# Moving one unit's loads forward in a fused RWKV-6 and feed-forward kernel, and reordering a few steps around it

## The chip, the cores and the metric

The kernel runs on one core of one Trainium2 chip. The metric is the device time of one execution in microseconds, as a median of several runs. The profile shows one execution; its span (675.3 us here) is a little shorter than the time of a run (677.92 us), because the run counts start and end as well.

## What is computed

Two blocks follow each other. The first is a linear attention with a state of 48 x 48 per head, 4 batches, 8 heads, 768 tokens:

```python
for t in range(S):
    cur = einsum('bhd,bhe->bhde', u * k[t], v[t])
    y[t] = einsum('bhd,bhde->bhe', r[t], state + cur)
    state = w[t][..., None] * state + einsum('bhd,bhe->bhde', k[t], v[t])
```

The second takes these outputs as x, 3072 tokens of 384 channels, through a feed-forward layer with weights of 384 x 2048 and 2048 x 384:

```python
h = x @ w_in
g = h * (1.0 / (1.0 + exp(-h)))
out = g @ w_out
```

All is in float32.

## The kernel before

The work is cut into 12 **units**, each of 128 tokens of two batches. In a unit the decays are multiplied up in seven levels, so that the recurrence becomes matrix products: at each level l the queries `tr` and keys `tk` are scaled by products `tw` of decays (VectorE and GpSimd), TensorE makes scores, and VectorE keeps the masked part of them. Then follow the outputs `yt`, the state's update, and the copies that bring `yt` into the layout of x (`xt`). The feed-forward layer of a unit runs on TensorE while the next unit's attention steps run on the other engines. While the first units run, the weights are rounded in 16 pieces ("piece": two steps on ScalarE, called head and tail, one join on VectorE, one add on GpSimd).

The loads of a unit from the third on come in blocks of 32 tokens. One call of `load_blocks` makes four transfers, and a unit needs twelve calls, so 48 transfers, all issued on the sync engine's queue:

```python
def load_blocks(i, name, g):
    n, b0 = units[i]
    src, t0 = {"w": w, "r": r, "k": k}[name], n * L + g * 32
    room = raw[:, i % NSLOT, WRK[name]]...          # two slots: units share one by parity
    for e in range(2):
        for a in range(2):
            nc.sync.dma_start(out=room[...], in_=src[...])

def block_loads(i):
    return [(load_blocks, i, name, g) for name in "wkr" for g in range(4)]
```

The same queue carries the weights, the outputs, the values, the tokens for the bonus term, its diagonal and the copies of x:

```python
def load_weight(i): ...; nc.sync.dma_start(out=dst, in_=src)         # L178
def load_rk(i): ...                                                  # L90, tokens for the bonus term
def bonus_sum(i, x): ...                                             # own_sums on VectorE, then at x == 1:
    for b in range(NB):
        for s in range(2):
            nc.sync.dma_start(out=diag[i][b][s::2], in_=own_sums[...])   # L423

def move_x(i):                                                       # ten transfers, L711
    xt[i] = pt.tile([128, KC, TU], F32, name="xt")
    for h in range(H):
        ...
        nc.sync.dma_start(out=xt[i][...], in_=yt[i][...])

def down(i, b, part, parts=4):                                       # unit 0's second product, in parts
    ...
    if part == parts - 1:
        nc.vector.tensor_copy(out=ob_b, in_=po[i, b])
        nc.sync.dma_start(out=out[row0:row0 + L, :], in_=ob_b)       # L777
```

Steps that the reading of the profile comes back to:

```python
def scores(i, l, *between):                 # products on TensorE (L525), then keep (L535) on VectorE
    ...
    if i < NTOK and grow: grow_queries(i, l)            # L471, VectorE
    do(*between)
    for e in range(2): keep(e)
def bonus_spread(i): ... ScalarE copies diag to both_b (L439, L441); VectorE shuffles it (L442)
def bonus_write(i):  ... copy_predicated into score (L448)
def turn(i, b, name): nc.vector.transpose(...)          # L336, raw -> tw, tk, tr
def turn_k(i, b):  transposes on TensorE; nc.scalar.copy(out=kq[i, b], in_=p_tr)     # L636
def y_state(i, b): p_yt = ps.tile(..., name="p_m", bufs=2); matmuls with state       # L648
def up(i, m):      12 matmuls xt, w_in -> p_h (L752); Silu on ScalarE (L758)
def sums(i, m), weight_sums(which): VectorE adds that prepare the second product     # L797, L789
def quarter(i, which): one of seven products of the second layer -> p_o, two buffers
                                                        # L815, evicted on VectorE, L824
```

From unit 3 on the order is regular: `mix(i)` gives thirteen groups of attention steps, and between them stand seven `quarter` steps of unit i - 2 and eight `up` steps of unit i - 1. The first three units are ordered by hand. The part that the change touches most, before:

```python
for m in range(6):
    do((piece, 10 + m), *others[m])          # unit 2's start; others[5] begins with (clear, 1)
...
others = {2: [(level, 2, 2), (prepare, 2, 3), (weight_sums, 1), (sums, 1, 0), (down, 0, 0, 3), (down, 0, 1, 0), (bonus, 2, 0),
              (bonus_sum, 2, 0)],
          3: [(burst, 2, 3), (keep_level, 2, 3), (keep_level, 2, 4), (go_on, 2, 4), (prepare, 2, 5), (down, 0, 1, 1),
              (bonus, 2, 1), (bonus, 2, 2), (load_rk, 3), (sums, 1, 1), (down, 0, 1, 2), (bonus_sum, 2, 1)],
          4: [(down, 0, 1, 3)],
          5: [(burst, 2, 5), ..., (bonus_spread, 2), (bonus_write, 2), (load_values, 3), (weight_sums, 2)],
          6: [(up, 1, 7), (sums, 1, 2)]}
loads = block_loads(3) + block_loads(4)
for l in range(2, NL):
    do(*others[l], *loads[(l - 2) * len(loads) // 5:(l - 1) * len(loads) // 5])
do(*both(turn_k, 2), (sums, 1, 3), *both(y_state, 2), *both(y, 2), (weight_sums, 3), *both(update, 2), (move_x, 2))
```

`clear(1)` sets the unused columns of the slot that units 1 and 3 share to zero; it has to come before unit 3's loads.

Of the kernel before, what the change touches and what calls it, by code (L numbers as in the profile page):

```python
# [38 lines left out]
def kernel(  # L39
# [11 lines left out]
    nc = tc.nc  # L51
# [4 lines left out]
    NL = 7  # L56
# [11 lines left out]
    NTOK = 2  # L68
# [387 lines left out]
    def odd_keys(i, l):  # L456

        c, blocks = 1 << l, NP * (L >> (l + 2))
        nc.scalar.copy(out=keys(i, X[(l + 1) % 2] * L + c, [4 * c, blocks], [c, 2], [1, c]),  # L459
                       in_=keys(i, NP * L + c, [4 * c, blocks], [NP * L + c, 2], [1, c]))  # L460
# [7 lines left out]
    def grow_queries(i, l):  # L468
        c = 1 << l
        odd = tr[i].rearrange("p q (i s c) -> p q i s c", s=2, c=c)[:, :, :, 1, :]  # L470
        nc.vector.tensor_tensor(out=odd, in0=odd, in1=tw[i][l][:, :, 0::2][:, :, :, None].to_broadcast([128, Q, L >> (l + 1), c]),  # L471
                                op=ALU.mult)
# [44 lines left out]
    def score_products(i, l, queries, sc):  # L517
        c, ni = 1 << l, L >> (l + 1)

        for p in range(NP):  # L520
            for e in range(2):
                rows = slice(PD * e, PD * e + D)

                apart, r_p, s_p = 2 * (NP - p) - 1, queries[rows, p, :], sc[e][:, p, :]
                nc.tensor.matmul(bass.AP(tensor=s_p.tensor, offset=s_p.offset,  # L525
                                         ap=[s_p.ap[0], [apart * L // 2, 2], [1, L // 2]]),
                                 lhsT=tk[i][rows, X[l % 2] + p, :],
                                 rhs=bass.AP(tensor=r_p.tensor, offset=r_p.offset + c,
                                             ap=[r_p.ap[0], [apart * L, 2], [2 * c, ni], [1, c]]),
                                 start=True, stop=True)  # L530

    def keep_masked(i, l, e, sc):
        c, ni = 1 << l, L >> (l + 1)
        dst = score[:, i % NSC, e].rearrange("p (b q) (i s c) -> p b q i s c", b=NB, s=2, c=c)[:, :, :, :, 1, :]
        nc.vector.copy_predicated(out=dst, mask=masks[l][:, :, None].to_broadcast([128, NB, NP, ni, c]),  # L535
                                  data=sc[e].rearrange("p (b q) (i c) -> p b q i c", b=NB, c=c))

    def scores(i, l, *between):
        c, ni = 1 << l, L >> (l + 1)

        name = "p_h" if i == 0 and l % 2 == 1 else "p_sc"
        sc = [ps.tile([128, Q, L // 2], F32, name=name, bufs=2) for e in range(2)]
        score_products(i, l, tr[i], sc)
        if i < NTOK and l + 2 < NL:
            odd_keys(i, l + 1)

        def keep(e):
            if (i, l, e) in COPIED:

                for b in range(NB):  # L550
                    for x in range(ni):
                        first = 2 * x * c if b == 0 else L - (2 * x + 1) * c
                        rows, columns = slice(first, first + c), slice((2 * x + 1) * c, (2 * x + 2) * c)
                        nc.scalar.copy(out=score[rows, i % NSC, e, b * NP:(b + 1) * NP, columns],
                                       in_=sc[e][rows, b * NP:(b + 1) * NP, x * c:(x + 1) * c])
                return
            keep_masked(i, l, e, sc)


        grow = l + 1 < NL or units[i][0] > 0  # L560
        if i < NTOK and grow:
            grow_queries(i, l)
        do(*between)
        for e in range(2):
            keep(e)
        if i >= NTOK and grow:
            grow_queries(i, l)

    def level(i, l):
        if l + 1 < NL:  # L570
            odd_keys(i, l)
        scores(i, l)
        grow_keys(i, l)
        add_weight()
# [140 lines left out]
    def both(fn, i, *args):  # L715
        return [(fn, i, b, *args) for b in range(NB)]

    def block_loads(i):
        return [(load_blocks, i, name, g) for name in "wkr" for g in range(4)]
# [122 lines left out]
    def do(*steps):  # L842
        for fn, *args in steps:
            fn(*args)
# [7 lines left out]
    def back(fn, i, *args):  # L852
# [8 lines left out]
    blocks = block_loads(2)  # L861
    others = {1: [(clear, 0), (beat, 6)], 2: [(turn, 1, 0, "r"), (head_weight, 0), (beat, 2)],
              3: [(turn, 1, 1, "r"), (head_weight, 1), (beat, 2)], 4: [(turn, 1, 1, "w"), (reverse_v, 0)],
              5: [(bonus_spread, 0), (bonus_write, 0), (turn, 1, 0, "w")], 6: [*both(turn_in, 1, "k"), *blocks[0:4], (tail_weight, 0)]}
    between = {4: [(bonus_sum, 0, 1)]}
    for l in range(1, NL):
        do((scores, 0, l, *between.get(l, ())), *[(grow_keys, 0, l + 1)] * (l + 1 < NL), *others[l])
# [2 lines left out]
       *blocks[4:8], (product, 1, 0), (tail_weight, 1), (turn_k, 0, 0), (join_weight, 1), (dense_x, 0, 0), (turn_k, 0, 1),  # L870
       *both(turn, 1, "k"), (dense_x, 0, 1), (grow_queries, 1, 0), (odd_ones, 1), (tail_weight, 2), (head_weight, 2),
       *blocks[8:12], (start_keys, 1, nc.gpsimd, True), (add_weight,), (up, 0, 0), (join_weight, 2),
       (start_keys, 1, nc.gpsimd, False), (add_weight,), (tail_weight, 3), (head_weight, 3), (odd_keys, 1, 1), (grow_keys, 1, 1),
       (scores, 1, 1, (join_weight, 3)), (add_weight,), (up, 0, 1), (tail_weight, 4), (grow_keys, 1, 2), (head_weight, 4),
       (up, 0, 2))


    others = {1: [], 2: [(bonus_sum, 1, 0), (bonus_sum, 1, 1), (load_rk, 2), *both(update, 0)],
              3: [(bonus_spread, 1), (reverse_v, 1), (load_values, 2)], 4: [(bonus_write, 1)], 5: []}

    def piece(i):

        do(*[(head_weight, i + 1)] * (i + 1 < 2 * NW), (join_weight, i), (add_weight,), *[(tail_weight, i + 1)] * (i + 1 < 2 * NW))

    for m in range(1, 5):
        do((piece, m + 3), (scores, 1, m + 1), *[(grow_keys, 1, m + 2)] * (m + 2 < NL), (up, 0, m + 2), *others[m])

    do((scores, 1, NL - 1), (head_weight, 9), (join_weight, 8), (add_weight,), (up, 0, 7), *both(y, 1), (turn_apart, 1),
       (tail_weight, 9), *both(turn_k, 1), *both(dense_x, 1), (piece, 9), *both(update, 1), (up, 1, 0), *both(turn, 2, "w"))

    others = {0: [(up, 1, 1), (down, 0, 0, 0), *both(turn, 2, "k"), (product, 2, 0), (product, 2, 1)],
              1: [(up, 1, 2), *both(turn, 2, "r"), *[(product, 2, l) for l in range(2, NL)]],
              2: [(down, 0, 0, 1), (odd_ones, 2), (start_keys, 2, nc.gpsimd, True), (grow_queries, 2, 0)],
              3: [(up, 1, 3), (start_keys, 2, nc.gpsimd, False), (reverse_v, 2)], 4: [(level, 2, 1), (up, 1, 4)],
              5: [(clear, 1), (down, 0, 0, 2), (up, 1, 5), (weight_sums, 0)]}
    for m in range(6):
        do((piece, 10 + m), *others[m])
    rounding.close()
    second.append(ctx.enter_context(tc.tile_pool(name="po", bufs=1, space=bass.MemoryType.PSUM)))

    others = {2: [(level, 2, 2), (prepare, 2, 3), (weight_sums, 1), (sums, 1, 0), (down, 0, 0, 3), (down, 0, 1, 0), (bonus, 2, 0),
                  (bonus_sum, 2, 0)],
              3: [(burst, 2, 3), (keep_level, 2, 3), (keep_level, 2, 4), (go_on, 2, 4), (prepare, 2, 5), (down, 0, 1, 1),
                  (bonus, 2, 1), (bonus, 2, 2), (load_rk, 3), (sums, 1, 1), (down, 0, 1, 2), (bonus_sum, 2, 1)],
              4: [(down, 0, 1, 3)],
              5: [(burst, 2, 5), (keep_level, 2, 5), (keep_level, 2, 6), (go_on, 2, 6), (up, 1, 6), (bonus_spread, 2),
                  (bonus_write, 2), (load_values, 3), (weight_sums, 2)],
              6: [(up, 1, 7), (sums, 1, 2)]}
    loads = block_loads(3) + block_loads(4)
    for l in range(2, NL):  # L910
        do(*others[l], *loads[(l - 2) * len(loads) // 5:(l - 1) * len(loads) // 5])
    do(*both(turn_k, 2), (sums, 1, 3), *both(y_state, 2), *both(y, 2), (weight_sums, 3), *both(update, 2), (move_x, 2))

    ROOM = 1, 1, 2, 1, 1, 1, 1, 1, 2, 1, 2, 1, 0
    for i in range(3, len(units)):
# [39 lines left out]
```

## Time and profile before

| | |
|---|---|
| time, median of 3 runs | 677.92 us (677.67 to 677.95) |
| span of the profiled execution | 675.3 us |
| TensorE (PE) busy | 648.6 us, 96% |
| VectorE (DVE) busy | 435.7 us, 65% |
| GpSimd (POOL) busy | 280.4 us, 42% |
| ScalarE (ACT) busy | 202.8 us, 30% |
| granted TensorE clock, mean | 0.982 |
| DMA | 49.21 MB, mean 73 GB/s |

A profile line of a timeline gives the start, the duration, the engine, the line of the kernel, the operation with out<-in, and how often it follows itself; in square brackets stands how long the engine was idle before it, and who released it. "SPq" is the sync engine's DMA queue: its durations are the time that the issuing takes, not the transfer. A line of windows gives the busy time of every engine in one stretch, and the granted clock of TensorE, where 1.00 is full speed. Busy time of TensorE counts slow matmuls as busy too, so a stretch at half clock looks busy and does half the work.

### The profile page before, as it was taken

Reading aid. Unit: us, or ns where it says so; the run is one execution under the profiler, and the core shown is the slowest. Engines: PE = TensorE matmul, PEld = TensorE weight load, DVE = VectorE, ACT = ScalarE, POOL = GpSimd, SP = SyncE. Lnnn points to the kernel's source line nnn. Section 1 sums busy time; section 2 is a strip of 40 time slices with the busy share of each in tenths; the row PEclk is TensorE's granted clock in tenths of the full one; section 3 lists DMA queues with packets and bytes.
Section 4 is the critical chain, followed back from the end, with each engine's and each line's share of the span. In section 5 each row is a group of like instructions: output and inputs, shape, how many; then the busy total and the mean of one; then the engine's idle time right before and its main releaser. Section 6 shows DMA issues by size and latency. Waiting matters only on the chain.

```text
span 675.3 us, 12894 instructions
## 1 busy us (share of the span) xinstructions
PE 648.6 (96%) x4878; PEld 585.1 (87%) x4878; DVE 435.7 (65%) x737; ACT 202.8 (30%) x408; POOL 280.4 (42%) x356
## 2 busy tenths in 40 slices
PE   8989999877599999999999999999999999999998
PEld 7877875777389989989989989989989989989997
DVE  6889779766147757757757757658658656653131
ACT  6787871210032132132132132123123133122110
POOL 6887489243205425425425425434434434330000
PEclk9999999889599999999999999999999999999999
DMA  9857911443353441441351451451451121100000
GB/s 235 252 92 225 239 50 26 81 74 48 64 106 52 70 86 33 68 90 33 62 96 31 64 98 28 64 96 29 65 96 32 33 49 26 47 2 24 23 1 24
DMA packets 201134, 49.21 MB, mean 73 GB/s; under 512 B 188912, under 2 KB 195952, under 8 KB 201072
## 3 DMA queue, kind: packets, MB, share of 16 engines
q1 hardware_dynamic: 199488, 47.79, 34.9%
q10 hardware_dynamic: 1584, 0.59, 0.4%
q8 instruction: 39, 0.64, 0.4%
q14 instruction: 23, 0.19, 0.1%
HBM read 39.52 MB, written 4.72 MB: 66 GB/s over the span
## 4 chain that ended last, share of the span: by engine, by line
PE 81%; DVE 7%; SPq 6%; issue 2%; ACT 2%; POOL 2%; DMA 1%; DVEq 0%; POOLq 0%; ACTq 0%
PE p_h L752 34%; PE p_o L815 27%; PE p_sc L525 5%; SPq L106 4%; PE p_m L525 3%; PE p_m L661 3%; PE p_m L648 2%; DVE score L535 2%; PE p_m L348 1%; DVE temps L797 1%; PE p_m L635 1%; DVE tr L471 1%; DVE own L789 1%; SPq L711 1%; PE p_sc L675 1%
## 5 line engine op out<-in xcount | busy, mean ns | idle before, releaser
L752 PE MATMUL p_h<-xt,w_in_sb 128*128 128x256 f32 x1152 | 262.1, 385 | 12.0 <-DMA xt<-yt 11.3
L752 PEld LDWEIGHTS p_h<-xt,w_in_sb 128*128 128x128 f32 x1152 | 217.8, 192 | 45.9 <-issue 12.8
L758 ACT ACTIVATE gt<-p_h 128x512 f32<-128x512 f32 x93 | 55.5, 596 | 239.7 <-PE p_h L752 239.6
L489 POOL TENSOR_TENSOR tk<-tk,tw 128x256 f32<-128x256 f32 x144 | 100.4, 720 | 41.7 <-ACT tk L459 24.7
L535 DVE COPY_PREDICATED score<-mask,p_sc 128x512 f32<-128x512 int8 x78 | 64.1, 885 | 75.6 <-PE p_sc L525 75.4
L815 PE MATMUL p_o<-own,temps 128*128 128x192 f32 x528 | 92.8, 334 | 4.3 <-DVE temps L824 4.3
L815 PEld LDWEIGHTS p_o<-own,temps 128*128 128x128 f32 x528 | 88.2, 194 | 5.7 <-DVE temps L824 4.6
L815 PE MATMUL p_o<-w_out_sb,gt 128*128 128x192 f32 x528 | 90.4, 328 | 0.0
L815 PEld LDWEIGHTS p_o<-w_out_sb,gt 128*128 128x128 f32 x528 | 85.9, 190 | 0.9 <-issue 0.4
L680 POOL TENSOR_TENSOR state<-state,tw 128x512 f32<-128x512 f32 x16 | 18.9, 1201 | 125.3 <-PE p_m L648 125.3
L384 POOL TENSOR_TENSOR tw<-tw 128x256 f32<-128x256 f32 (+6 forms) x83 | 37.7, 454 | 56.0 <-DVE tw L336 52.1
L797 DVE TENSOR_TENSOR temps<-gt 128x256 f32<-128x256 f32 x88 | 45.2, 513 | 21.4 <-ACT gt L758 21.4
L525 PEld LDWEIGHTS p_sc<-tr,tk 48*128 48x128 f32 x640 | 39.5, 186 | 14.0 <-issue 8.5
L471 DVE TENSOR_TENSOR tr<-tr,tw 128x512 f32<-128x512 f32 x53 | 49.8, 940 | 2.7 <-PE p_h L525 0.7
L459 ACT COPY tk<-tk 128x256 f32<-128x256 f32 x60 | 24.5, 409 | 88.2 <-PE p_sc L525 43.1
L525 PE MATMUL p_sc<-tr,tk 48*128 48x128 f32 x640 | 47.5, 285 | 2.2 <-DVE score L535 1.5
L406 POOL TENSOR_TENSOR ruk<-tokens_rk 128x768 f32<-128x768 f32 x10 | 18.1, 1814 | 68.7 <-DVE own_sums L413 68.7
L591 DVE TENSOR_TENSOR tr<-tr,tw 128x512 f32<-128x512 f32 x29 | 36.4, 1256 | 0.4
L824 DVE TENSOR_TENSOR partial<-p_o,partial 128x192 f32<-128x192 f32 x33 | 11.7, 354 | 37.9 <-PE p_o L815 37.9
L535 DVE COPY_PREDICATED score<-mask,p_m 128x512 f32<-128x512 int8 x54 | 35.4, 706 | 0.0
L505 POOL TENSOR_TENSOR tk<-tk,tw 128x128 f32<-128x128 f32 x44 | 32.0, 760 | 2.3 <-ACT tk L495 1.8
L815 PE MATMUL p_o<-w_out_sb,temps 128*128 128x192 f32 x176 | 30.4, 326 | 0.0
(144 smaller groups left out, 745.3 us busy)
## 6 DMA issues: line engine op xcount, KB each, us to landing
w_out_sb<-in_moe_w_in_dram SPq DMA_DIRECT2D x6, 768.0 KB, 7.0
tokens_rk<-in_r_dram SPq DMA_DIRECT2D x20, 192.0 KB, 3.4
tokens_rk<-in_k_dram SPq DMA_DIRECT2D x20, 192.0 KB, 3.7
w_out_sb<-in_moe_w_out_dram SPq DMA_DIRECT2D x4, 768.0 KB, 5.6
own<-in_moe_w_out_dram SPq DMA_DIRECT2D x4, 768.0 KB, 6.8
xt<-yt SPq DMA_DIRECT2D x60, 48.0 KB, 2.0
raw<-in_w_dram SPq DMA_DIRECT2D x80, 32.0 KB, 2.2
raw<-in_k_dram SPq DMA_DIRECT2D x80, 32.0 KB, 2.3
```

Source lines behind the costliest of these rows:

```text
L106: nc.sync.dma_start(out=room[(2 * e + a) * 32:(2 * e + a + 1) * 32, :, g, 0:d1 - d0], in_=src[b0:b0 + NB, e::2, t0:t0 + 32, d0:d1].rearran ...
L384: engine.tensor_tensor(out=up, in0=t[:, :, 0::2], in1=t[:, :, 1::2], op=ALU.mult)
L471: nc.vector.tensor_tensor(out=odd, in0=odd, in1=tw[i][l][:, :, 0::2][:, :, :, None].to_broadcast([128, Q, L >> (l + 1), c]), op=ALU.mult)
L489: nc.gpsimd.tensor_tensor(out=out, in0=have, in1=odd_products(i, l, b, *blocks), op=ALU.mult)
L505: engine.tensor_tensor(out=keys(i, X[1] * L + 3 * b, [4, n], [1, 1]) if own else have, in0=have, in1=odd_products(i, 0, b, [4, n], skip=2 ...
L525: nc.tensor.matmul(bass.AP(tensor=s_p.tensor, offset=s_p.offset, ap=[s_p.ap[0], [apart * L // 2, 2], [1, L // 2]]), lhsT=tk[i][rows, X[l % ...
L535: nc.vector.copy_predicated(out=dst, mask=masks[l][:, :, None].to_broadcast([128, NB, NP, ni, c]), data=sc[e].rearrange("p (b q) (i c) -> ...
L591: nc.vector.tensor_tensor(out=new[:, :, :, 1, :], in0=old[:, :, :, 1, :], in1=tw[i][l][:, :, 0::2][:, :, :, None].to_broadcast([128, Q, L ...
L752: nc.tensor.matmul(p_h[:, a, :], lhsT=w_in_sb[:, c, f * 128:(f + 1) * 128], rhs=xt[i][:, c, :], start=(c == 0), stop=(c == KC - 1))
L758: nc.scalar.activation(out=gt[i, m], in_=p_h, func=AF.Silu)
L797: nc.vector.tensor_tensor(out=out, in0=one, in1=two, op=op)
L815: nc.tensor.matmul(p, lhsT=left(f), rhs=right[:, f, :], start=(f == 0), stop=(f == FH - 1))
```

## The change

Unit 3's block loads (the fourth unit's) are issued during the last pieces of weights, right behind the last weights on the sync queue. Unit 4's loads go into unit 2's later steps, and the last five of their twelve calls go behind `move_x(2)`, the copies of x of the third unit. For this, `clear(1)` moves to an earlier step. Some steps in units 1 and 2 change places: at level 1 of unit 1 the join of a weight comes before the growing of the queries; copies of odd keys come before a weight's head; at level 5 the growing of the keys comes before a weight's add; one part of `down` and the `bonus_sum` steps come earlier. The same operations run with the same operands. The core of the diff (the removed `others` of units 2 and 3 stand above):

```diff
-        if i < NTOK and grow:
+        if i == 0 and grow:
             grow_queries(i, l)
         do(*between)
+        if i == 1 and grow:
+            grow_queries(i, l)
...
-       ..., (tail_weight, 3), (head_weight, 3), (odd_keys, 1, 1), (grow_keys, 1, 1),
+       ..., (tail_weight, 3), (odd_keys, 1, 1), (head_weight, 3), (grow_keys, 1, 1),
...
-              3: [(bonus_spread, 1), (reverse_v, 1), (load_values, 2)], 4: [(bonus_write, 1)], 5: []}
+              3: [(bonus_spread, 1), (reverse_v, 1), (clear, 1), (load_values, 2)]}
...
-    for m in range(1, 5):
-        do((piece, m + 3), (scores, 1, m + 1), *[(grow_keys, 1, m + 2)] * (m + 2 < NL), (up, 0, m + 2), *others[m])
+    for m in range(1, 4):
+        do((piece, m + 3), (scores, 1, m + 1), (grow_keys, 1, m + 2), (up, 0, m + 2), *others[m])
+    do((head_weight, 8), (join_weight, 7), (scores, 1, 5), (grow_keys, 1, 6), (add_weight,), (tail_weight, 8), (up, 0, 6),
+       (bonus_write, 1))
...
+    blocks = block_loads(3)
-              1: [..., *[(product, 2, l) for l in range(2, NL)]],
+              1: [..., *[(product, 2, l) for l in range(2, NL)], *blocks[0:3]],
-              2: [..., (grow_queries, 2, 0)],
+              2: [..., (grow_queries, 2, 0), *blocks[3:6]],
-              3: [..., (reverse_v, 2)], 4: [(level, 2, 1), (up, 1, 4)],
+              3: [..., (reverse_v, 2), *blocks[6:9]], 4: [(level, 2, 1), (up, 1, 4), *blocks[9:12]],
-              5: [(clear, 1), (down, 0, 0, 2), (up, 1, 5), (weight_sums, 0)]}
+              5: [(down, 0, 0, 2), (up, 1, 5), (weight_sums, 0)]}
...
-    loads = block_loads(3) + block_loads(4)
-    for l in range(2, NL):
-        do(*others[l], *loads[...])
-    do(..., *both(update, 2), (move_x, 2))
+    blocks = block_loads(4)
+    do(*blocks[0:2], (level, 2, 2), (prepare, 2, 3), (weight_sums, 1), (down, 0, 1, 0), (down, 0, 0, 3), (down, 0, 1, 1),
+       (sums, 1, 0), (bonus, 2, 0), (bonus_sum, 2, 0))
+    do(blocks[2], (burst, 2, 3), (keep_level, 2, 3), (keep_level, 2, 4), (go_on, 2, 4), (prepare, 2, 5), (bonus, 2, 1),
+       (bonus, 2, 2), (down, 0, 1, 2), (bonus_sum, 2, 1), (load_rk, 3), (sums, 1, 1), *blocks[3:7], (down, 0, 1, 3))
+    do((burst, 2, 5), (keep_level, 2, 5), (keep_level, 2, 6), (go_on, 2, 6), (up, 1, 6), (bonus_spread, 2), (bonus_write, 2),
+       (load_values, 3), (weight_sums, 2), (up, 1, 7), (sums, 1, 2))
+    do(*both(turn_k, 2), (sums, 1, 3), *both(y_state, 2), *both(y, 2), (weight_sums, 3), *both(update, 2), (move_x, 2),
+       *blocks[7:])
```

More of the change, by code (lines that the diff above doesn't have):

```diff
@@ L872 @@
        *blocks[8:12], (start_keys, 1, nc.gpsimd, True), (add_weight,), (up, 0, 0), (join_weight, 2),
-       (start_keys, 1, nc.gpsimd, False), (add_weight,), (tail_weight, 3), (head_weight, 3), (odd_keys, 1, 1), (grow_keys, 1, 1),
+       (start_keys, 1, nc.gpsimd, False), (add_weight,), (tail_weight, 3), (odd_keys, 1, 1), (head_weight, 3), (grow_keys, 1, 1),
        (scores, 1, 1, (join_weight, 3)), (add_weight,), (up, 0, 1), (tail_weight, 4), (grow_keys, 1, 2), (head_weight, 4),
@@ L878 @@
     others = {1: [], 2: [(bonus_sum, 1, 0), (bonus_sum, 1, 1), (load_rk, 2), *both(update, 0)],
-              3: [(bonus_spread, 1), (reverse_v, 1), (load_values, 2)], 4: [(bonus_write, 1)], 5: []}
+              3: [(bonus_spread, 1), (reverse_v, 1), (clear, 1), (load_values, 2)]}
     def piece(i):
         do(*[(head_weight, i + 1)] * (i + 1 < 2 * NW), (join_weight, i), (add_weight,), *[(tail_weight, i + 1)] * (i + 1 < 2 * NW))
-    for m in range(1, 5):
-        do((piece, m + 3), (scores, 1, m + 1), *[(grow_keys, 1, m + 2)] * (m + 2 < NL), (up, 0, m + 2), *others[m])
+    for m in range(1, 4):
+        do((piece, m + 3), (scores, 1, m + 1), (grow_keys, 1, m + 2), (up, 0, m + 2), *others[m])
+    do((head_weight, 8), (join_weight, 7), (scores, 1, 5), (grow_keys, 1, 6), (add_weight,), (tail_weight, 8), (up, 0, 6),
+       (bonus_write, 1))
     do((scores, 1, NL - 1), (head_weight, 9), (join_weight, 8), (add_weight,), (up, 0, 7), *both(y, 1), (turn_apart, 1),
        (tail_weight, 9), *both(turn_k, 1), *both(dense_x, 1), (piece, 9), *both(update, 1), (up, 1, 0), *both(turn, 2, "w"))
+    blocks = block_loads(3)
     others = {0: [(up, 1, 1), (down, 0, 0, 0), *both(turn, 2, "k"), (product, 2, 0), (product, 2, 1)],
-              1: [(up, 1, 2), *both(turn, 2, "r"), *[(product, 2, l) for l in range(2, NL)]],
-              2: [(down, 0, 0, 1), (odd_ones, 2), (start_keys, 2, nc.gpsimd, True), (grow_queries, 2, 0)],
-              3: [(up, 1, 3), (start_keys, 2, nc.gpsimd, False), (reverse_v, 2)], 4: [(level, 2, 1), (up, 1, 4)],
-              5: [(clear, 1), (down, 0, 0, 2), (up, 1, 5), (weight_sums, 0)]}
+              1: [(up, 1, 2), *both(turn, 2, "r"), *[(product, 2, l) for l in range(2, NL)], *blocks[0:3]],
+              2: [(down, 0, 0, 1), (odd_ones, 2), (start_keys, 2, nc.gpsimd, True), (grow_queries, 2, 0), *blocks[3:6]],
+              3: [(up, 1, 3), (start_keys, 2, nc.gpsimd, False), (reverse_v, 2), *blocks[6:9]], 4: [(level, 2, 1), (up, 1, 4), *blocks[9:12]],
+              5: [(down, 0, 0, 2), (up, 1, 5), (weight_sums, 0)]}
     for m in range(6):
@@ L899 @@
     second.append(ctx.enter_context(tc.tile_pool(name="po", bufs=1, space=bass.MemoryType.PSUM)))
[L901 to L908, printed above, removed]
-    loads = block_loads(3) + block_loads(4)
-    for l in range(2, NL):
-        do(*others[l], *loads[(l - 2) * len(loads) // 5:(l - 1) * len(loads) // 5])
-    do(*both(turn_k, 2), (sums, 1, 3), *both(y_state, 2), *both(y, 2), (weight_sums, 3), *both(update, 2), (move_x, 2))
+    blocks = block_loads(4)
[7 more added lines that the diff above has]
+       *blocks[7:])
     ROOM = 1, 1, 2, 1, 1, 1, 1, 1, 2, 1, 2, 1, 0
```

## The prediction

> **What bounds the kernel now.** I read the page's slices first, then the busy table by windows, then TensorE's timeline, and last the sync queue's own timeline and the chain of waits. The slices say that TensorE is at 9 tenths nearly everywhere, with a hole in slices 8 to 11 (118 to 186 us), where the granted clock falls too. The windows give the size of hole and steady state (columns: window, length, PE, weight loads, DVE, ACT, POOL, clock, DMA share, GB/s):
>
> ```profile
> 136.00:165.00 29.00, 24.70 (x174) 23.63 (x172) 17.63 (x32) 3.52 (x7) 11.15 (x18) 0.88 0.44 62
> 165.00:179.00 14.00, 2.70 (x8) 1.24 (x6) 6.53 (x8) 0.00 (x0) 5.56 (x4) 0.68 0.33 55
> 191.00:242.00 51.00, 51.00 (x394) 47.20 (x396) 34.74 (x59) 12.55 (x28) 21.09 (x28) 1.00 0.41 72
> 242.00:293.00 51.00, 51.00 (x396) 47.20 (x396) 34.84 (x59) 12.54 (x28) 21.01 (x28) 1.00 0.36 63
> ```
>
> From 191 us on, TensorE is busy for all of 51 us per unit at clock 1.00, and the chain of waits repeats the same pieces every 50.9 us to the end. Nothing there is touched by the change, so what moves is when this train starts. Its first piece, the up-projection of unit 2, is late. TensorE's timeline (start, duration, and in brackets the wait and who ended it):
>
> ```profile
> 129.29 3.54 PE L648 MATMUL p_m<-tr,state 128*128 128x128 f32 x16 [2.75 <-ACT kq L636]
> ...
> 140.67 2.76 PE L815 MATMUL p_o<-own,temps 128*128 128x192 f32 x16
> 147.73 5.41 PE L815 MATMUL p_o<-own,temps 128*128 128x192 f32 x16 [4.30 <-DVE temps L824]
> ...
> 174.30 1.19 PE L752 MATMUL p_h<-xt,w_in_sb 128*128 128x256 f32 x2 [9.18 <-DMA xt<-yt]
> 176.73 1.19 PE L752 MATMUL p_h<-xt,w_in_sb 128*128 128x256 f32 x2 [1.24 <-DMA xt<-yt]
> 178.80 3.75 PE L752 MATMUL p_h<-xt,w_in_sb 128*128 128x256 f32 x8 [0.87 <-DMA xt<-yt]
> ```
>
> Three holes: A at 126.5, B at 143.4, C from 165.1. After each, the same shape takes twice as long (5.41 against 2.76). The sync queue tells why:
>
> ```profile
> 80.81 3.90 SPq L178 DMA_DIRECT2D own<-in_moe_w_out_dram  x2
> 111.83 0.37 SPq L777 DMA_DIRECT2D out_dram<-temps  x1
> 112.29 7.81 SPq L106 DMA_DIRECT2D raw<-in_w_dram  x16
> 120.20 1.86 SPq L90 DMA_DIRECT2D tokens_rk<-in_r_dram  x2
> 122.10 1.31 SPq L90 DMA_DIRECT2D tokens_rk<-in_k_dram  x2
> 123.51 2.49 SPq L423 DMA_DIRECT2D diag<-own_sums  x4
> ...
> 163.09 7.85 SPq L106 DMA_DIRECT2D raw<-in_r_dram  x16
> 171.03 6.27 SPq L711 DMA_DIRECT2D xt<-yt  x10
> ```
>
> The queue stands idle from 84.7 to 111.8, waiting to write an output, and then issues 96 block loads in one row at 7.85/16 = 0.49 us each, 47 us in all. The ten copies of x (L711) stand behind them, though yt was ready at 135.4 (start 134.76 plus 0.59 in ACT's timeline). That is hole C. Hole B is the same queue: VectorE's transpose of unit 3's r waited for its load.
>
> ```profile
> 144.95 1.30 DVE L336 STREAM_TRANSPOSE tr<-raw 128x512 f32<-128x512 f32 x2 [2.60 <-DMA raw<-in_r_dram]
> 128.32 0.01 DVE L442 LOAD_MASK_SELECT both_b<-both_b  x1 [4.07 <-ACT both_b L441]
> ```
>
> The second line is behind hole A: own_sums was ready at 120.8, but its diag copies left only at 123.5, behind the block and token loads, and ACT's in-order copies to kq stood behind the wait for diag.
>
> **What the Trainium skill says.** "TensorE: Matmul & The Clock Gate", Part 1: the array runs at half rate after an idle window of about 3.4 us and needs about as long under load to return. The trace agrees on the half (clock 0.50 to 0.52 in two-microsecond windows after holes B and C, 5.41 against 2.76 us), though here a wait of 2.75 us was enough; waits of 0.58 to 0.74 us cost no clock. "DMA: Bandwidth & Descriptors", Rules for kernel authors: issue a DMA early, compute, wait late. The change is that. The same page, Issuing engines are not separate DMA queues, calls the sequencer's time to start a DMA usually small beside the DMA; here it is what limits (0.49 us an issue, 96 in a row). "GPSIMD Engine Reference", Specifications: GpSimd shares its SBUF interfaces with VectorE, in contention with two-input instructions. The trace agrees: L471 takes 0.68 us alone and 2.33 us beside a GpSimd add. So work that moves between those two has no fixed cost.
>
> **The change part by part.** No instruction is added or removed; all is order. Work left over by TensorE's holes, against full speed:
> - A: 2.75 of wait, and 3.54 - 1.78 (the same 16 matmuls in the steady state) = 1.76. Sum 4.5.
> - B: 4.30, and 5.41 - 2.76 = 2.65. Sum 6.95.
> - C: 9.18, and the 48 up matmuls took from 174.30 to 190.93 = 16.63 against 10.56 in the steady state, 6.07 more. Sum 15.25.
> - D: short waits before that, 0.39 + 0.70 + 0.30 + 0.15 between 46 and 66 us and 0.58 at 104 us. Sum 2.1.
>
> All: 28.8 us. What the new order leaves of them:
>
> *Unit 3's 48 issues move to 84.7.* Their room was emptied early in unit 1, and its clearing moves from 97 us to a place at about 62 us where ACT waited 2.6 us for weights. They end at 84.7 + 48 x 0.49 = 108.2. Eight issues for unit 4 end at 112.1, the output at 112.5, four more at 114.5. All before own_sums.
>
> *own_sums moves ahead of four sums on VectorE* (117.58 to 119.83, 2.2 us): ready at 118.5 instead of 120.8. Diag issues 2.5, landing 1.9: 122.9 instead of 127.3. With ACT's five copies (about 1.2) and the shuffle, VectorE's wait ends at about 124.8 instead of 128.5. ACT reaches kq when the transposes are done (126.5), so y_state starts at about 126.9: **A leaves 0.4** and no loss of clock. Gain 4.1.
>
> *Hole B becomes VectorE's own work.* From the bonus write (128.52) to the end of the eviction that TensorE waited for (147.31 + 0.36) are 19.15 us, of them 2.60 wait for r. So 124.8 + 16.55 = 141.3. TensorE went from 129.29 to 143.43 = 14.14, of them 1.76 slow clock: 126.9 + 12.4 = 139.3. It still waits **2.0 us**. Whether that drops the clock, no row here tells (0.87 no, 2.75 yes); I take 3 in 10, of 2.65: 0.8. Gain 6.95 - 2.0 - 0.8 = 4.1.
>
> *The copies of x.* After diag at 121.0: token loads 3.2, 16 block issues 7.8, output 0.4, five value loads 2.4: 134.8. Ten copies 6.3, landing 2.0: 143.1. TensorE wants them at 141.3 + 14.7 (147.73 to 165.12, less 2.65 slow clock) = 156. **C leaves nothing**, with 13 us to spare. Gain 15.25. Twenty issues of unit 4 follow, 9.8 us, to 151, and unit 4 turns at about 183 only.
>
> *The small orders.* A down part ahead of the last one fills the 0.58 us wait for the last rounded weight. Keys ahead of a weight's add on GpSimd at level 5, and the join ahead of the queries' product at level 1, aim at the other 1.5; VectorE has the same sum of work there and the contention moves, so I count 0.5. Gain 1.1.
>
> Sum: 4.1 + 4.1 + 15.25 + 1.1 = **24.6 us**; 677.9 - 24.6 = **653.3 us**, 3.6% less. From the end: the up matmuls of unit 2 end at 156 + 10.56 = 166.6 instead of 190.93, 24.3 earlier, plus the 1.1, less the 0.8. The same.
>
> **Rivals.**
> 1. *VectorE takes the place of the queue.* From 93 to 124 us it is busy without a pause (19.86 of 20 us between 100 and 120), and hole B shows that it stays last. For it: all of that. Against: it has 16 us idle of 51 in each steady unit, so it catches up within unit 3. If its chain came 3 us later than I reckon, B is 5 us and half clock: 657 to 659.
> 2. *The queue stays the bound*, because an in-order wait (the output, the token loads, diag) holds it up as the output did at 111.8. For it: that one wait lasted 27 us. Against: now the long loads stand ahead of it, and there are 13 us to spare. Only a new wait of over 13 us would show; then 660 or more.
> 3. *The holes close wholly*, with VectorE 2 us faster than reckoned (its two contended sums, 1.26 and 1.15 against 0.41, beside GpSimd's state product): B zero, 650.
> 4. *Early loads collide with the last weights* (own lands 3.85 us after its issue). Those weights are issued first and in the same queue; VectorE and ACT reach them at 90 us and later. A loss of 1 us at most.
> 5. *It was hidden anyway.* Not so: the chain of waits runs through the sync queue's issues, nearly all L106 and L711, from 136.5 to 176.7.
>
> **Range and chances.** The low end, 650, is nearly everything gained (677.9 - 28.8 = 649.1). The high end, 659, is B unimproved at half clock (2.85 worse) and a further 3 us in A and D. Over 2% faster means under 664.4, where a gain of 13.5 suffices; C alone gives 15.25. I say 0.95.
>
> **What the profile after would show.** Lines from 525 on stand two higher. Right: L106 of unit 3 at about 85 to 108 without a pause; diag at 118 to 119; L713 at about 135, ending with no wait in front of L754; slices 8 to 11 at clock 9; units of 50.9 us as before; a wait of about 2 us at L817, on temps. Wrong: a wait in front of L754 on xt (queue), over 3 us at L817 (VectorE), a new wait of L525 on tk or tr in unit 3, or units longer than 51 us (unit 4's or 5's loads late). What would make it wrong most: a clock that falls at the 2 us wait, or VectorE's chain between 60 and 124 us shifted by the small orders.

## The result and the profile after

The changed kernel takes **653.3 us** (652.56 to 654.02) against 677.91 us, a ratio of 0.9638 (95% interval 0.9621 to 0.9654): 24.6 us less. The profiled span went from 675.3 to 651.6 us.

The page's slices after, TensorE and its granted clock:

```profile
PE   8999999989999999999999999999999999999998
PEclk9999999999999999999999999999999999999999
```

The hole in slices 8 to 11 is gone. The windows say the same for the stretch from 136 to 165 us, where TensorE was busy for 24.70 us at clock 0.88 before, and for a later unit, which is as full as it was:

```profile
136.00:165.00 29.00, 26.44 (x186) 24.37 (x185) 20.05 (x32) 6.14 (x12) 18.80 (x26) 1.00 0.41 71
219.00:270.00 51.00, 51.00 (x397) 47.20 (x396) 34.87 (x59) 12.50 (x27) 21.05 (x28) 1.00 0.36 64
```

TensorE's timeline after: one line of unit 1, the places of holes A, B and C, and one line of unit 4 (lines behind the first edit stand two higher):

```profile
72.18 2.94 PE L701 MATMUL p_m<-yt,ruk 128*128 128x128 f32 x24 [0.66 <-ACT yt L667]
...
125.66 2.05 PE L650 MATMUL p_m<-tr,state 128*128 128x128 f32 x16 [0.29 <-ACT kq L638]
...
140.87 2.87 PE L817 MATMUL p_o<-own,temps 128*128 128x192 f32 x16 [2.56 <-DVE temps L826]
...
155.65 10.63 PE L754 MATMUL p_h<-xt,w_in_sb 128*128 128x256 f32 x48
...
192.73 2.87 PE L817 MATMUL p_o<-own,temps 128*128 128x192 f32 x16 [0.65 <-DVE temps L826]
```

A shrank to 0.29 us, B to 2.56, and the up-projection at C starts with no bracket at all: 48 matmuls in one piece, at full speed. They end at 166.3 instead of 190.9 us. The first and the last line are waits that the kernel before did not have. The sync queue after:

```profile
80.59 3.91 SPq L178 DMA_DIRECT2D own<-in_moe_w_out_dram  x2
84.55 8.87 SPq L106 DMA_DIRECT2D raw<-in_w_dram  x16
93.47 8.98 SPq L106 DMA_DIRECT2D raw<-in_k_dram  x16
102.49 7.84 SPq L106 DMA_DIRECT2D raw<-in_r_dram  x16
110.38 3.90 SPq L106 DMA_DIRECT2D raw<-in_w_dram  x8
114.38 0.39 SPq L779 DMA_DIRECT2D out_dram<-temps  x1
...
118.64 2.79 SPq L423 DMA_DIRECT2D diag<-own_sums  x4
...
137.06 6.58 SPq L713 DMA_DIRECT2D xt<-yt  x10
...
171.56 2.44 SPq L423 DMA_DIRECT2D diag<-own_sums  x4
```

The 27 us in which the queue stood idle are filled with unit 3's loads, diag leaves 4.9 us earlier, and the copies of x leave at 137 instead of 171.

### The profile page after: what moved, and what is told of

Read it like the earlier page. It is cut to its first block, busy times and chain, and to the rows that moved or that the text cites. A ratio compares the mean times of both kernels' runs of the same rounds, so it can differ in the third digit from the quotient of the medians.

```text
span 651.6 us, 12886 instructions
## 1 busy us (share of the span) xinstructions
PE 640.5 (98%) x4878; PEld 579.4 (89%) x4878; DVE 431.5 (66%) x737; ACT 203.1 (31%) x408; POOL 281.0 (43%) x356
## 4 chain that ended last, share of the span: by engine, by line
PE 84%; SPq 5%; DVE 3%; DMA 2%; ACT 2%; issue 2%; POOL 1%; DVEq 0%; POOLq 0%; ACTq 0%
PE p_h L754 33%; PE p_o L817 29%; PE p_sc L525 6%; PE p_m L525 4%; SPq L106 3%; PE p_m L773 2%; PE p_m L663 2%; PE p_m L650 2%; PE p_m L348 2%; PE p_m L637 1%; DMA w_out_sb<-in_moe_w_in_dram 1%; SPq L90 1%; DMA w_out_sb<-in_moe_w_out_dram 1%; PE p_m L852 1%; POOL tk L489 1%
## 5 line engine op out<-in xcount | busy, mean ns | idle before, releaser
L754 PE MATMUL p_h<-xt,w_in_sb 128*128 128x256 f32 x1152 | 258.2, 382 | 0.7 <-POOL tk L505 0.7
L754 PEld LDWEIGHTS p_h<-xt,w_in_sb 128*128 128x128 f32 x1152 | 215.8, 190 | 32.6 <-POOL tk L505 0.9
L817 PE MATMUL p_o<-own,temps 128*128 128x192 f32 x528 | 90.5, 328 | 3.2 <-DVE temps L826 3.2
L817 PEld LDWEIGHTS p_o<-own,temps 128*128 128x128 f32 x528 | 85.8, 190 | 4.9 <-DVE temps L826 3.8
L471 DVE TENSOR_TENSOR tr<-tr,tw 128x512 f32<-128x512 f32 x53 | 47.3, 893 | 2.7 <-PE p_sc L525 0.8
L593 DVE TENSOR_TENSOR tr<-tr,tw 128x512 f32<-128x512 f32 x29 | 35.9, 1237 | 0.4
```

What stands on the lines that cost most here:

```text
L593: nc.vector.tensor_tensor(out=new[:, :, :, 1, :], in0=old[:, :, :, 1, :], in1=tw[i][l][:, :, 0::2][:, :, :, None].to_broadcast([128, Q, L ...
L754: nc.tensor.matmul(p_h[:, a, :], lhsT=w_in_sb[:, c, f * 128:(f + 1) * 128], rhs=xt[i][:, c, :], start=(c == 0), stop=(c == KC - 1))
L817: nc.tensor.matmul(p, lhsT=left(f), rhs=right[:, f, :], start=(f == 0), stop=(f == FH - 1))
```

## The experiments

Theory 1: the gain is idle time of the sync queue put to use; diag, unit 3's loads and the copies of x all come earlier by it, and what is left is VectorE's own chain in unit 3. Against it stand: only the order counts (copies first); the small orders in unit 1 carry the gain; the places behind have slack. The kernels of one group ran on one chip beside the kernel before.

### First group: parts undone

**Unit 1's small orders put back** (the early loads stay):

```diff
-        if i == 0 and grow: ...   do(*between)   if i == 1 and grow: ...
+        if i < NTOK and grow: grow_queries(i, l)   # then do(*between)
-  (odd_keys, 1, 1), (head_weight, 3)
+  (head_weight, 3), (odd_keys, 1, 1)
-  (head_weight, 8), (join_weight, 7), (scores, 1, 5), (grow_keys, 1, 6), (add_weight,), (tail_weight, 8), (up, 0, 6)
+  (piece, 7), (scores, 1, 5), (grow_keys, 1, 6), (up, 0, 6)
```

> The changed kernel with the three small orders of unit 1 put back as they were before (queries before the join at level 1, the weight's head before the odd keys, the weight's add before the keys of level 5). All moved loads stay. Theory 1 (the sync queue's order is the cause): 653.3 + 0.5 = 653.8 us, between 653 and 655; the short waits of TensorE at 46 to 48 and 65 to 66 us come back, 1.5 us in all, and part of that is lost again behind them. Rival (the small orders carry through VectorE's chain to the wait in unit 3): 655.5 us or more, and the wait on temps in unit 3 is over 3.5 us.

Measured: 653.4 us (652.59 to 654.14), ratio 0.9643 (0.9627 to 0.9659). The short waits came back (0.39, 0.70 and 0.32 us in its profile), but the time didn't move by more than its scatter, and the wait in unit 3 was 2.55 us. The small orders of unit 1 don't carry the gain. In return the wait of 0.66 us for yt at 72 us is gone: this profile has 1.41 us of short waits, the changed kernel's 1.27 (0.61 and 0.66). In these two profiles one short wait stands in the place of another, but the changed kernel run again below had only one of 0.59 us there. Whether the small orders bring half a microsecond or nothing, these runs can't tell.

**The copies of x behind the last loads of unit 4:**

```diff
-       (weight_sums, 3), *both(update, 2), (move_x, 2), *blocks[7:])
+       (weight_sums, 3), *both(update, 2), *blocks[7:], (move_x, 2))
```

> The changed kernel with the ten copies of x of unit 2 put behind the last five calls (20 issues, 10.9 us in the profile) of unit 4's loads. Theory 1 (the copies have about 12 us of slack, so that their place alone is not what counts): the copies start at 148 instead of 137, the last lands at 156.5, TensorE wants it at 155.65; about 1 us longer, 653 to 655.5 us. Rival (the place of the copies ahead of unit 4's loads is the gain): 10 us longer, 663 us.

Measured: 653.25 us (651.53 to 654.3), ratio 0.9646 (0.9626 to 0.9666): no change. Its sync queue, and its TensorE at hole C:

```profile
145.75 6.78 SPq L713 DMA_DIRECT2D xt<-yt  x10
```

```profile
154.74 10.63 PE L754 MATMUL p_h<-xt,w_in_sb 128*128 128x256 f32 x48
```

The copies leave nearly 9 us later than in the changed kernel, and TensorE, which reaches L754 at 154.74, still doesn't wait. So the slack is real, and the part of the edit that puts the copies ahead of five calls is worth nothing by itself.

**Copies first, but the idle time unused:**

```diff
-    blocks = block_loads(3)          # and its four places behind the last weights
...
-    blocks = block_loads(4)
+    blocks = block_loads(3)          # in the same places, the last five calls ahead of load_values(3)
...
-       *both(update, 2), (move_x, 2), *blocks[7:])
+       *both(update, 2), (move_x, 2), *block_loads(4))
```

> The changed kernel without the early issue: unit 3's loads stand where unit 4's stand in the changed kernel (two calls at the start of unit 2's later steps, the rest spread, the last five ahead of the values), and all of unit 4's loads stand behind the copies of x. So the copies of x still come ahead of unit 4's loads, but most of the queue's idle time from 85 to 112 us isn't used. Theory 1 (the gain is that idle time put to use, about 24 us of issuing): unit 3's r arrives at about 144 instead of 108, the wait in unit 3 is about 8 us at least, with slow clock behind it, and the queue is still behind in units 3 and 4: 665 to 685 us. Rival (order is enough, the copies first): within 2 us of 653.

Measured: 677.2 us in its only run, the time of the kernel before (677.27 beside it). All of the gain is gone, though the copies of x stand ahead of unit 4's loads. Queue, TensorE and ScalarE of this version:

```profile
83.59 4.92 SPq L106 DMA_DIRECT2D raw<-in_w_dram  x8
106.91 0.37 SPq L779 DMA_DIRECT2D out_dram<-temps  x1
...
194.11 2.45 SPq L423 DMA_DIRECT2D diag<-own_sums  x4
```

```profile
147.12 5.49 PE L817 MATMUL p_o<-own,temps 128*128 128x192 f32 x16 [9.74 <-DVE temps L826]
199.18 5.18 PE L754 MATMUL p_h<-xt,w_in_sb 128*128 128x256 f32 x12 [13.14 <-ACT gt L760]
```

```profile
196.57 0.20 ACT L439 COPY both_b<-diag 128x16 f32<-128x16 f32 x1 [15.95 <-DMA diag<-own_sums]
```

From 88.5 to 106.9 us the queue is idle again, as before the change. Hole C is still closed, but its time shows up elsewhere: 9.74 us in unit 3, for r, and 13.14 us later in unit 3, at the last step of unit 2's up-projection, because unit 3's diag now leaves at 194 behind everything else, and ScalarE, in order, holds Silu behind it. Moving one wait on a full queue makes another.

This order alone gains nothing. But the run changes two things at once: unit 3's loads are late, and all 48 loads of unit 4 stand ahead of unit 3's diag. The 48 matmuls at L754 ended at 175.2 here, 8.9 us later than in the changed kernel, but still 15.7 us earlier than in the kernel before (190.9). The wait of 13.14 us and the slow matmuls behind it (5.18 us against 2.76) took these 15.7 us back. Whether an order with unit 3's diag ahead of unit 4's loads would keep that part of the gain, without using the idle time, is not shown.

**One VectorE sum done twice** (1.74 us more in unit 3's chain, same result):

```diff
-       (load_values, 3), (weight_sums, 2), (up, 1, 7), (sums, 1, 2))
+       (load_values, 3), (weight_sums, 2), (weight_sums, 2), (up, 1, 7), (sums, 1, 2))
```

> The changed kernel with one weight sum on VectorE done twice (same result), 1.74 us more in the chain that TensorE waits for in unit 3. The wait of 2.56 us becomes 4.3. Theory 1 (VectorE's chain ends last there, and unit 4 has 0.65 us of wait that takes up part of it): 1.1 us longer if the clock holds (654.4), 3.7 us if the clock halves behind the wait as it did before (657.0); a wait of 4.3 us lost the clock before, so 657. Rival (something else than VectorE ends last, such as GpSimd or a load): no change, 653.3.

Measured: 655.97 us (655.5 to 656.54), 2.7 longer, between the two numbers. The wait is 4.33 us as expected, and the clock fell, but the matmuls behind it took 4.55 us instead of 2.87, a loss of 1.68 and not of the 2.65 that hole B cost before. 1.77 of wait and 1.68 of clock, less the 0.65 us that unit 4 no longer waits, make 2.8. VectorE's chain does end last in unit 3: the wait grew by as much as the sum takes.

```profile
142.16 4.55 PE L817 MATMUL p_o<-own,temps 128*128 128x192 f32 x16 [4.33 <-DVE temps L826]
```

### Second group: what is left after the change

**VectorE's chain shortened in two places:**

```diff
-       (bonus_sum, 2, 1), (load_rk, 3), (sums, 1, 1), *blocks[3:7], ...
+       (sums, 1, 1), (bonus_sum, 2, 1), (load_rk, 3), *blocks[3:7], ...
-       *both(y, 2), (weight_sums, 3), *both(update, 2), ...
+       *both(y, 2), *both(update, 2), ...      # and, for unit 3:
+        if i == 3: groups[2].insert(1, (weight_sums, 3))
```

> The changed kernel with two pieces of VectorE work moved off the chain that TensorE waits for in unit 3: four sums of unit 1 ahead of own_sums of unit 2, where VectorE waited 1.7 us for GpSimd, and the last weight sum (1.75 us) into unit 3, where VectorE waited 2.0 us. The wait of 2.56 us goes to zero. Theory 1 (unit 4 is still timed by the sync queue, whose diag of unit 3 left at 171.6 though own_sums was ready at 162.2): the time comes back as a wait in unit 4, which grows from 0.65 to 3.2 us: 653.3, within 1 us, or 2.6 us more if the clock halves there. Rival (VectorE's chain in unit 3 is the last thing): 650.7 us.

Measured: 653.04 us (652.45 to 654.24), ratio 0.9645 (0.9631 to 0.9659): no gain, as theory 1 said, but only in part for its reason. The wait in unit 3 went only to 1.67 us, and unit 4's grew to 1.45 (0.73 for gt and 0.72 on temps) and not to 3.2. VectorE's timeline of this version, with one line of GpSimd's ahead of it, has the cause:

```profile
115.02 2.13 POOL L408 TENSOR_TENSOR ruk<-ruk,u_bc 128x768 f32<-128x768 f32 x1
...
115.41 2.03 DVE L799 TENSOR_TENSOR temps<-gt 128x256 f32<-128x256 f32 x1
117.47 0.72 DVE L799 TENSOR_TENSOR temps<-temps,gt 128x256 f32<-128x256 f32 x1
...
126.93 2.59 DVE L791 TENSOR_TENSOR own<-w_out_sb 128x1536 f32<-128x1536 f32 x1
```

A sum that takes 0.42 us alone took 2.03 beside GpSimd's product of ruk (115.0 to 117.2), the next one 0.72 beside a product of keys, and the weight sum 2.59 instead of 1.74 beside GpSimd's state product. Own_sums came about 1 us late by it, diag too, and TensorE waited 0.81 us for kq instead of 0.29. Unit 3's diag left at 171.54, as in the changed kernel (171.56), though L754 of unit 2 began 1.2 us earlier (154.42; 0.9 us of that TensorE had already at 118 us): what was gained up to there came back in unit 4, as theory 1 says, but it was too little to decide between the theory and its rival.

**Unit 5's loads behind unit 3's diag:**

```diff
-        behind = groups[2:]
+        behind = groups[9:] if i == 3 else groups[2:]
```

> The changed kernel with unit 5's loads in unit 3 put behind the diag copies (into the last four groups of steps instead of the last eleven). Theory 1: diag leaves at about 162 to 164 instead of 171.6, VectorE's wait for both_b of 5.6 us shrinks to about the 2.1 us of later units, and the wait of 0.65 us in unit 4 is gone: 652.7 us. Rival (the wait of 0.65 us has another cause, or the copies of x of unit 3 now come late): no change, or longer by over 1 us.

Measured: 652.36 us (652.21 to 653.38), ratio 0.9636 (0.9623 to 0.9649). Diag leaves at 161.52, VectorE's longest wait for both_b falls from 5.6 to 2.9 us, and unit 4 has no wait. The size is right, but it is within the scatter, and neither the copies behind the loads above nor the changed kernel run again below waited in unit 4 (their diag left at 169.21 and 168.10): the 0.65 us is there in some executions only.

**Both together** (the two diffs above in one kernel):

> The two before together. Theory 1 (VectorE in unit 3, the sync queue in unit 4): both waits go, 2.56 + 0.65 = 3.2 us, 650.1 us, that is more than the two parts alone add up to (0 and 0.6). Rival (VectorE alone in unit 3): the same 650.7 as without the queue's part.

Measured: 651.24 us (650.87 to 653.0), ratio 0.9616 (0.9603 to 0.9629). The waits left are 0.82 for kq and 1.69 in unit 3, so the expected 650.1 isn't reached, for the same reason: four sums in the wrong company. Beside the version with VectorE's chain shortened alone it is 1.8 us faster, and unit 4 has no wait, which agrees with theory 1. Its profiled run is its slowest: ScalarE waited 4.12 us for a weight there (2.04 in the changed kernel's profile), and TensorE 1.73 us at 68 to 69.5 us behind it. That is one source of the scatter of these kernels.

### Third group: the better version, the scatter, and diag by itself

**The last weight sum later, unit 5's loads behind diag, the four sums left where they were:**

```diff
-       *both(y, 2), (weight_sums, 3), *both(update, 2), ...
+       *both(y, 2), *both(update, 2), ...      # and, for unit 3:
+        if i == 3: groups[2].insert(1, (weight_sums, 3))
...
-        behind = groups[2:]
+        behind = groups[9:] if i == 3 else groups[2:]
```

> The run before (both parts) without the four sums moved ahead of own_sums, because there they ran beside GpSimd's adds and took 4.0 us instead of 1.7, which made own_sums and diag 1.1 us late. So: the last weight sum in unit 3, and unit 5's loads behind diag. Theory 1: the wait for kq is back at 0.3 us, the wait on temps in unit 3 is 2.56 - 1.75 = 0.8, none in unit 4: 653.3 - 1.75 - 0.65 = 650.9 us, and about 0.5 us less than the version with both parts, run beside the others. Rival (only work moved away from GpSimd's neighbourhood counts, this sum isn't last): the wait stays at 2.5 us, 652.4 us as with the diag order alone.

Measured: 650.58 us (650.16 to 653.72), ratio 0.9614 (0.9595 to 0.9633). TensorE in unit 3:

```profile
138.64 2.87 PE L817 MATMUL p_o<-own,temps 128*128 128x192 f32 x16 [0.90 <-DVE temps L826]
```

2.56 - 1.75 = 0.81 was expected, 0.90 came, and kq is back at 0.29. The version before differs from this one in the four sums alone, which stand ahead of own_sums there, as in the kernel before the change: 0.82 + 1.69 us of waits against 0.29 + 0.90. So this part of the change, own_sums ahead of the sums, is worth about 1.3 us by the waits. Beside the changed kernel on the same chip (652.69) it is 2.1 us faster; the two intervals overlap, but four of its five runs lie below every run of the other.

**The changed kernel again** (no edit):

> The changed kernel itself, beside the others of this call, as a measure of its scatter: 653.3 us, between 652.5 and 654.2, because the weights of the start land up to 1 us earlier or later from run to run.

Measured: 652.69 us, ratio 0.9647 (0.9619 to 0.9676). Three runs at a mean clock of 1.000 took 650.8, 651.97 and 652.04, two at 0.997 took 653.33 and 653.39. One took 658.29 at 0.995; no profile of it exists, and its cause stays open. Its profiled run has the same wait as the profile above, and not the same matmuls behind it:

```profile
139.98 4.55 PE L817 MATMUL p_o<-own,temps 128*128 128x192 f32 x16 [2.56 <-DVE temps L826]
```

4.55 against 2.87 us behind the same 2.56 us of wait: the clock falls in one execution and not in the other. The two groups of times, about 1.8 us apart in the mean, fit the 1.68.

**Diag late, all else as changed:**

```diff
-       (bonus_sum, 2, 1), (load_rk, 3), (sums, 1, 1), *blocks[3:7], ...
+       (load_rk, 3), *blocks[3:5], (bonus_sum, 2, 1), (sums, 1, 1), *blocks[5:7], ...
```

> The changed kernel with the tokens for the bonus term and two calls of unit 4's loads (12 issues, about 6.5 us) put ahead of unit 2's diag copies, as they stood before the change. Everything else stays, the early loads too. Theory 1 (VectorE and ScalarE both wait for diag, so its place on the queue is on the path by itself): VectorE's bonus write and ScalarE's kq both come 6 us later, TensorE waits about 6 us ahead of y_state and then runs slow for 1.8; the wait in unit 3 is then about 1.3 us and the one in unit 4 gone: 659 us, between 657.5 and 661. Rival (what VectorE does after it has slack, or the wait in unit 3 takes it up): 656.8 us or less.

Measured: 658.4 us (657.74 to 659.56), ratio 0.9722 (0.9703 to 0.9741), about 5.4 us more than the mean of the changed kernel's two medians (653.0). Its sync queue, and its TensorE at hole A:

```profile
125.89 2.46 SPq L423 DMA_DIRECT2D diag<-own_sums  x4
```

```profile
131.44 3.79 PE L650 MATMUL p_m<-tr,state 128*128 128x128 f32 x16 [5.37 <-ACT kq L638]
```

7.2 us later on the queue are 5.1 us more wait (5.37 against 0.29) and 1.74 of slow clock (3.79 against 2.05); the wait in unit 3 shrinks from 2.56 to 1.23, because TensorE is late itself. The place of four small transfers on the queue is worth more than 5 us.

## Why the prediction was right

- **What bounds the kernel.** Right. From the end of unit 2's up matmuls to the end of the span are 484.4 us before and 485.3 after; all of the gain lies ahead of it.
- **Unit 3's 48 issues from 84.7 to 108.2.** They ran from 84.55 to 110.33, 0.54 us each and not 0.49, because the first 32 went slower (8.87 and 8.98 for 16). It cost nothing: own_sums was what diag waited for.
- **Hole A.** Diag was foreseen at 118.5, it left at 118.64; TensorE's wait 0.4 and 0.29. The late-diag run shows that this step is a cause by itself. That the time of diag was met so closely is partly luck: VectorE came to own_sums at 116.4 and then waited for GpSimd's product, which the prediction didn't have. The loss of clock behind hole A was also a little smaller than the 1.76 us counted: in the timeline, from which the 3.54 comes, the same 16 matmuls take 1.95 in a later unit, which makes 1.6.

```profile
118.06 1.01 DVE L417 TENSOR_REDUCE own_sums<-ruk 128x8 f32<-128x384 f32 x2 [1.70 <-POOL ruk L408]
```

- **Hole B.** Foreseen as VectorE's own chain with 2.0 us left; it was 2.56, because TensorE came to it 1.0 us earlier than reckoned (138.3 and not 139.3) and VectorE 0.5 (140.8 and not 141.3). Doubling a sum lengthened it by as much as the sum takes. The clock was put at 3 chances in 10 of losing 2.65 us, 0.8. Both factors were off and their product was not: over the runs of the five kernels with this wait, 12 of 22 have a mean clock of 0.997 or less, and the one profiled loss behind it was 1.68; if all twelve lost that, it makes 0.9. The prediction's bound from below, a wait of 0.87 us without loss, can't be read from its line: the clock was at half there already (8 matmuls in 3.75 us, where 48 take 10.63 at full clock).
- **Hole C.** Gone, with the copies at 137 instead of 134.8. The slack was about 10 us and not 13 (the last copy issued by 143.6, 2.0 us to landing, wanted at 155.65), and the run with the copies behind the loads used up nearly all of it and lost nothing. But the step named the copies as what C waited for, and the run with the idle time unused shows that they are only its last link: there they were ahead of unit 4's loads and C was closed, and the same time came back for r and for diag.
- **The small orders.** 1.1 us were counted, 0.5 of them for unit 1, which is smaller than the scatter and neither confirmed nor refuted; the profile shows 1.27 us of waits there instead of 1.54. The wait of 0.58 us at 104 is gone.
- **The range.** Its high end took 2.85 us for a hole B that doesn't improve; that is what was to be left of it. Unimproved, B costs the 4.1 us that were counted as its gain, and the high end would have been about 660.
- **What it missed.** The wait of 0.66 us for yt in unit 1, and the wait of 0.65 us in unit 4. For the latter, the prediction checked the queue in unit 3 for unit 4's loads, and not for unit 3's diag, which left 9.4 us after own_sums was ready (162.2). Rival 2, the queue stays the bound, was right in this small part.

The end of the up matmuls was foreseen at 166.6 and came at 166.3. That the median hits 653.3 to the tenth is luck at a scatter of about 1 us.

## What to carry to other kernels

Where many small transfers share one in-order queue, add up its issues as the work of an engine: here about 0.5 us for a block load and 0.65 for a copy of x. Look for the time in which the queue waits in order for something unrelated (27 us for one output), and put transfers that are already free to go ahead of that wait. Small transfers with a reader on the path (four for diag) belong ahead of bulk, and moving one of them forward on a full queue only helps if another one doesn't take its place at the end. When work is moved on VectorE, look at what GpSimd does at the place where it goes.

## What was not expected of the hardware

A wait of TensorE of 2.56 us cost the clock in one execution of a kernel and not in another, and what it cost was 1.68 us. In the profiles, from 30 us on, waits of 1.73 us and less at full clock showed no loss: the 16 matmuls behind a wait of 1.67 us took 2.87 us, as behind one of 0.65. One run of 653.72 us of the version with the wait of 0.90 us had a mean clock of 0.997 all the same; no profile of it exists.

A sum of 0.42 us on VectorE took 2.03 us beside a GpSimd product, nearly five times as long; in the kernel before, one of 0.68 us had taken 2.33. In the two versions that have this sum beside the product, it ended 0.3 us after the product did (117.44 and 117.15; 119.12 and 118.84). So what it lost there was the rest of the product, and not a fixed factor.
